# Where the stores wait: early stores on ScalarE's queue or held behind transposes, and a few softmax steps listed elsewhere

## The chip, the core and the metric

The kernel runs on one core of a Trainium2 chip. The metric is the device time of one execution in microseconds (us); the median of three runs of the kernel before is 420.4 us (419.74 to 420.79). The profile was taken on another execution of the same kernel, which took 418.92 us; its span from the first to the last instruction is 417.1 us, and all times inside the profile are counted from the start of that span.

The core has five engines with a queue of instructions each: TensorE (PE) multiplies matrices, VectorE (DVE) and ScalarE (ACT) do elementwise work, GpSimd (POOL) and SyncE (SP) here mainly start DMA transfers. A DMA can be started from the queues of SP, ACT or POOL.

## The reference, cut

```python
# 8 batches x 4160 positions x 192 channels (8 heads x 24 channels), kernel of 7 taps
w = exp(weight_gen - max(weight_gen, axis=-1))      # [B, S, 8, 7]
w = w / (sum(w, axis=-1) + 1e-09)
x_pad = concatenate([zeros(B, 6, D), x], axis=1)
x_unf = x_pad[:, idx, :].reshape(B, S, 7, 8, 24)    # position s sees s .. s + 6 of x_pad
out = einsum('bshk,bskhg->bshg', w, x_unf)          # a dynamic convolution
x = out.reshape(33280, 192)
g = maximum(x @ w1, x @ w2)                         # 192 -> 1024
result = g @ w_out                                  # 1024 -> 192, float32
```

The kernel writes maximum(h1, h2) as h1 + relu(h2 - h1): the hidden product is x @ (w2 - w1), then a relu, then its product with w_out, to which x @ (w1 @ w_out) is added.

## The kernel before: what the change touches

The 33,280 tokens are laid out as 128 partitions x 260 columns. The 260 columns form 17 *batches* b of 16 columns (the last has 4). DVE and the transposes work by *units* u: batches 0 and 1 have four units of 4 columns (u = 0 to 7), batches 2 to 15 two units of 8 columns (u = 8 to 35), batch 16 one unit of 4 (u = 36). The hidden products go by *tiles* t, one for each column (260), in *groups* g: pairs of tiles up to tile 15 (groups 0 to 7), then three tiles each (group 8 is tiles 16 to 18, group g is tiles 3g - 8 to 3g - 6). In each group two or four columns of the output are computed as well, some tiles behind.

For each batch the softmax is four steps on ACT and DVE, listed by hand at certain tiles: `exp_sum` (ACT), `red` (DVE), `ln` (ACT), `shift` (DVE), and `weights` (ACT), the final exp, once for each half-batch. Then DVE multiplies (`mul`) and adds (`adds`) to y. A DMA transposes y to yt, on SP's queue, and PE uses yt.

```python
    def exp_sum(b):                                              # ACT
        e_ts[b] = pe_.tile([P, BATCHES[b][1] * WGC], FP32, name="e_t", tag="e")
        nc.scalar.activation(out=e_ts[b], in_=wg_ts[b], func=AF.Exp)
    # ...
    def weights(b, o):                                           # ACT, line 158: en_t <- wg_t
        # ...
    def mul(b, o):                                               # DVE, line 173: m_t <- xb_t, en_t
        # ...
    def transpose(u):
        b, o, n = UNITS[u]
        yt = pyt.tile([P, 8 // 2 * 3 * P], BF16, name="yt", tag="yt")
        nc.sync.dma_start_transpose(                             # SP, line 207: yt <- y_t
            out=yt[:, 0:n // 2 * 3 * P].rearrange("p (b t) -> p b t", t=P),
            in_=y_ts[b][:, o * D:(o + n) * D],
        )
        yt_ts[u] = yt
        while held:
            held.pop(0)()

        nc.gpsimd.tensor_copy(out=gate, in_=yt[:, 0:1])          # POOL, line 215: waits for the landing
        c = b + 1 if o == 0 else b + 2
        if o == 8 and c < NB:
            load_x(c, 0, min(8, BATCHES[c][1]))
        if o == 0 and c < NB and BATCHES[c][1] > 8:
            load_x(c, 8, BATCHES[c][1] - 8)
        if o == 0 and b + 3 < NB:
            load_wg(b + 3, nc.gpsimd)
```

`transpose(u + 1)` is listed early in unit u, from unit 8 on (the first eight units are transposed by PE). The outputs are copied from PSUM by ACT and stored when a unit is complete:

```python
    def evac(p, n):
        # ... ACT, line 371: o_t <- op_ps, 24 columns of o_t are used in turn
        stores = []
        for q in range(p, p + n):
            u, i, _ = column(2 * q)
            if u < NU - 1 and i == UNITS[u][2] // 2 - 1:
                stores.append((nc.sync, place(q)[0] - i, [1, 2 * (i + 1) * D]))
            if u == NU - 1:
                stores.append((nc.sync, place(q)[0], [2 * D, 2], [1, D]))
        for eng, c, *ap in stores:
            def issue(eng=eng, c=c, ap=ap, o=o):
                eng.dma_start(                                   # line 383: out_dram <- o_t
                    # ...
                )
            if 8 <= u < NU - 3:
                held.append(issue)
            else:
                while held:
                    held.pop(0)()
                issue()
```

A group: PE does the hidden tiles but the last, then the first half of the outputs, then the last tile, then the second half. In a group with four output columns the listed steps (`beside`) come before the last relu and the eviction, in one with two after them:

```python
    def hidden(g, now=(), between=lambda: None, beside=lambda: None):
        t0, n = GROUPS[g]
        rd = room(g)
        for t in range(t0, t0 + n - 1):
            hid_tile(t)                                          # PE, line 275: hd <- yt, wd
        if now:
            out_room(now, "ab" if n == 1 and "ab" in ps else None)
            last = out_first(now)                                # PE, lines 327 and 315
        # ... relu of these tiles (ACT, line 285)
        hid_tile(t0 + n - 1)
        if len(now) > 2:
            beside()
        relu(rd, t0 + n - 1, 1)
        between()
        if now:
            out_second(now, go)                                  # PE, line 315
            evac(now[0] // 2, len(now) // 2)
        if len(now) <= 2:
            beside()
```

The tiles at which the softmax steps are listed, and the rule that puts off a long step in a group with four columns when the group before had a long one:

```python
    due = {}
    for c in range(3, NB):
        soon = c < 5
        parts_ = [(16 * (c - 2) + (8 if soon else 10), True, lambda c=c: weights(c, 0))]
        if 8 in dict(pieces(c)):
            parts_.append((16 * (c - 2) + (14 if soon else 15), True, lambda c=c: weights(c, 8)))
        if c > 3:
            ln_at = -2 if c == 4 else 0 if c < 8 else 2 if c < 11 else 4
            parts_.append((16 * (c - 2) + ln_at, False, lambda c=c: ln(c)))
            parts_.append((16 * (c - 3) + (4 if c == 4 else 7), True, lambda c=c: exp_sum(c)))
        for t, *step in parts_:
            due.setdefault(t, []).append(step)
    # ...
        two = len(OUTS[g]) <= 2
        put_off = [w for w in waiting if w[0] and not two and long_in_two[0]]
        now = [w for w in waiting if w not in put_off]
        waiting[:] = put_off
        for _, step in now:
            step()
        long_in_two[0] = two and any(long for long, _ in now)
```

Of the kernel before, what the change touches and what calls it, by code (L numbers as in the profile page):

```python
# [17 lines left out]
def _sub(base: bass.AP, off: int, dims):  # L18
    ap = [list(base.ap[0])] + [[int(s), int(c)] for s, c in dims]
    return dataclasses.replace(base, offset=base.offset + off, ap=ap)  # L20
# [3 lines left out]
def kernel(  # L24
# [9 lines left out]
    nc = tc.nc  # L34

    B, S, D = x.shape
# [13 lines left out]
    NB = len(BATCHES)  # L50


    def pieces(b):
        n = BATCHES[b][1]
        at, done = [], 0
        for w in (4, 4, 4, 4) if b < 2 else (8, 8) if n == 16 else (n,):
            at.append((done, w))
            done += w
        return at
# [65 lines left out]
    def exp_sum(b):  # L125
        e_ts[b] = pe_.tile([P, BATCHES[b][1] * WGC], FP32, name="e_t", tag="e")
        nc.scalar.activation(out=e_ts[b], in_=wg_ts[b], func=AF.Exp)  # L127
# [13 lines left out]
    def ln(b):  # L141
        nc.scalar.activation(out=s_ts[b], in_=s_ts[b], func=AF.Ln)  # L142
# [7 lines left out]
    def weights(b, o):  # L150

        w = dict(pieces(b))[o]
        if b not in en_ts:
            en_ts[b] = pen.tile([P, 16 * WGC * 2], BF16, name="en_t", tag="en")
        J = 2 if w == 4 and b < 2 else 1
        N = w * H // J
        for j in range(J):
            nc.scalar.activation(  # L158
                out=_sub(en_ts[b], (o * WGC + j * N * K) * 2, [[2 * N, K], [2, N], [1, 2]]),
                in_=_sub(wg_ts[b], (o * H + j * N) * K, [[1, K], [K, N], [0, 2]]), func=AF.Exp,  # L160
            )
# [90 lines left out]
    held = []  # L252
# [35 lines left out]
    def column(c):  # L288

        b = min(c // 16, NB - 1)  # L290
        for u, (ub, o, n) in enumerate(UNITS):
            if ub == b and o <= c - BATCHES[b][0] < o + n:
                k = c - BATCHES[b][0] - o
                return u, k // 2, k % 2

    def place(p):

        u, i, _ = column(2 * p)
        b, o, n = UNITS[u]
        return BATCHES[b][0] + o + i, n // 2  # L300
# [52 lines left out]
    def evac(p, n):  # L353

        tile_, at = op_at[p]
        o = o_t[0]
        if p == NT // 2 - 1:

            for j, copy, eng in ((0, nc.scalar.copy, nc.scalar), (1, nc.vector.tensor_copy, nc.sync)):
                c = place(p)[0] + 2 * j  # L360
                copy(out=o[:, c % 24 * D:(c % 24 + 1) * D], in_=tile_[:, at + j * 512:at + j * 512 + D])  # L361
                eng.dma_start(
                    out=bass.AP(tensor=out.tensor, offset=c * D, ap=[[CPP * D, P], [1, D]]),
                    in_=o[:, c % 24 * D:(c % 24 + 1) * D],
                )
            return
        runs = [[q for q in range(p, p + n) if column(2 * q)[0] == u]
                for u in range(column(2 * p)[0], column(2 * (p + n - 1))[0] + 1)]
        for qs in runs:
            c, h = place(qs[0])  # L370
            nc.scalar.copy(out=_sub(o, c % 24 * D, [[D, len(qs)], [h * D, 2], [1, D]]),  # L371
                           in_=_sub(tile_, at + (qs[0] - p) * D, [[D, len(qs)], [512, 2], [1, D]]))
        stores = []
        for q in range(p, p + n):
            u, i, _ = column(2 * q)
            if u < NU - 1 and i == UNITS[u][2] // 2 - 1:
                stores.append((nc.sync, place(q)[0] - i, [1, 2 * (i + 1) * D]))
            if u == NU - 1:
                stores.append((nc.sync, place(q)[0], [2 * D, 2], [1, D]))
        for eng, c, *ap in stores:  # L380

            def issue(eng=eng, c=c, ap=ap, o=o):
                eng.dma_start(
                    out=bass.AP(tensor=out.tensor, offset=c * D, ap=[[CPP * D, P], *ap]),
                    in_=_sub(o, c % 24 * D, ap),
                )

            if 8 <= u < NU - 3:
                held.append(issue)
            else:  # L390
                while held:
                    held.pop(0)()
                issue()

# [7 lines left out]
    OUTS, c = [[], [], []], 0  # L402
# [6 lines left out]
    NU = len(UNITS)  # L409
# [24 lines left out]
# [6 lines that stand above are left out]
            hid_tile(t)  # L440
        if now:
            out_room(now, "ab" if n == 1 and "ab" in ps else None)
            last = out_first(now)
        if len(now) > 2:
            relu(rd, t0, n - 1)
        else:
            for t in range(t0, t0 + n - 1):
                relu(rd, t, 1)
        if now:
            go = relay(last)  # L450
# [6 lines that stand above are left out]
            out_second(now, go)  # L457
# [4 lines that stand above are left out]
    def rest_of_results(c):  # L462

        parts = [p for p in (c[:4], c[4:-2], c[-2:]) if p]
        assert max(map(len, parts)) <= 4
        go = []
        for i, now in enumerate(parts):
            out_room(now, ("r", "ab", "c")[i])
            go.append(relay(out_first(now)))
            if i:  # L470
                out_second(parts[i - 1], go[i - 1])
                evac(parts[i - 1][0] // 2, len(parts[i - 1]) // 2)
        out_second(parts[-1], go[-1])
        evac(parts[-1][0] // 2, len(parts[-1]) // 2)
# [201 lines left out]

    due = {}
    for c in range(3, NB):
        soon = c < 5
        parts_ = [(16 * (c - 2) + (8 if soon else 10), True, lambda c=c: weights(c, 0))]  # L680
        if 8 in dict(pieces(c)):
            parts_.append((16 * (c - 2) + (14 if soon else 15), True, lambda c=c: weights(c, 8)))
        if c > 3:
            ln_at = -2 if c == 4 else 0 if c < 8 else 2 if c < 11 else 4
            parts_.append((16 * (c - 2) + ln_at, False, lambda c=c: ln(c)))
            parts_.append((16 * (c - 3) + (4 if c == 4 else 7), True, lambda c=c: exp_sum(c)))
        for t, *step in parts_:
            due.setdefault(t, []).append(step)
    waiting, long_in_two = [], [False]
# [87 lines left out]
```

The softmax here doesn't subtract the row's maximum and nothing guards it: scores larger than these inputs give would overflow.

## Time and profile before

| Engine | Busy us | Share of the span | Instructions |
|---|---|---|---|
| PE | 396.4 | 95% | 7369 |
| DVE | 377.2 | 90% | 218 |
| ACT | 359.2 | 86% | 424 |
| POOL | 84.2 | 20% | 102 |

| DMA issue | Queue | Count | KB each | Median us to landing |
|---|---|---|---|---|
| stores, 8 columns | SP | 28 | 768 | 4.9 |
| stores, 4 columns | SP | 8 | 384 | 2.6 |
| transposes yt <- y_t | SP | 29 | | 3.7 |

Busy time says how long an engine had an instruction under way; matmuls are pipelined, so a busy PE may still be waiting in part. The chain of waits in the profile puts 58% of the span on DVE and 24% on PE. In the profile, an engine's name with a q (SPq, ACTq) is its queue of DMA issues; a number in square brackets after an instruction is its engine's idle time before it, with what ended it. A line of the table of waits reads: who waited, for what, us in total, how often, the longest.

### The profile page before, as it was taken

The numbers are of one execution on the slowest core, as the hardware profiler recorded it, in microseconds if no ns is written. First come the engines' busy times: TensorE is split into PE (matmuls) and PEld (weight loads), VectorE is DVE, ScalarE is ACT, GpSimd is POOL, SyncE is SP. The second block draws the span as 40 slices with busy tenths as digits, with TensorE's granted clock in tenths as the row PEclk, the third lists the DMA queues.
The fourth block names the chain that finished last, engine by engine and source line by source line (L and its number), as shares of the span: only waits on it lengthen the run. The fifth ranks groups of instructions, "written<-read, shape, count | busy, mean of one in ns | idle before, by whom it ended". The sixth has DMA issues, their size and how long they took to land.

```text
span 417.1 us, 16029 instructions
## 1 busy us (share of the span) xinstructions
PE 396.4 (95%) x7369; PEld 320.9 (77%) x7369; DVE 377.2 (90%) x218; ACT 359.2 (86%) x424; POOL 84.2 (20%) x102
## 2 busy tenths in 40 slices
PE   7769899979999999999999999999999999989995
PEld 7668799767777778777787777777777777767795
DVE  5999999997989999999999999999999999999000
ACT  5888998969998999889898899998998989877871
POOL 1510101454113122220112222211221222210000
PEclk9999999999999999999999999999999999999999
DMA  8965425697663974766686587477639647544413
GB/s 249 258 166 160 108 78 79 152 191 195 158 143 73 269 181 77 238 178 123 115 240 168 123 220 174 103 204 206 140 92 256 164 64 235 151 87 116 172 55 137
DMA packets 60242, 65.68 MB, mean 157 GB/s; under 512 B 47601, under 2 KB 48497, under 8 KB 60176
## 3 DMA queue, kind: packets, MB, share of 16 engines
q1 hardware_dynamic: 51904, 40.47, 34.9%
q0 software_dynamic: 8128, 24.11, 27.9%
q8 instruction: 57, 0.93, 0.9%
q10 hardware_dynamic: 144, 0.10, 0.1%
q14 instruction: 9, 0.07, 0.1%
HBM read 35.96 MB, written 25.56 MB: 147 GB/s over the span
## 4 chain that ended last, share of the span: by engine, by line
DVE 58%; PE 24%; ACT 7%; issue 6%; DMA 4%; SPq 1%; DVEq 0%; ACTq 0%
DVE m_t L173 29%; DVE m_t L189 13%; PE op_ps L315 11%; PE hd L275 10%; DVE m_t L195 8%; ACT rd_t L285 3%; DVE sum_t L139 3%; DVE wg_t L147 2%; PE op_ps L327 2%; DVE y_t L198 2%; DMA yt<-y_t 2%; DMA ws1T<-in_moe_w_dram 2%; ACT en_t L158 1%; ACT yt L246 1%; ACT o_t L371 0%
## 5 line engine op out<-in xcount | busy, mean ns | idle before, releaser
L285 ACT ACTIVATE rd_t<-hd 128x1024 bf16<-128x1024 f32 (+1 forms) x206 | 234.7, 1188 | 29.8 <-PE hd L275 28.4
L315 PE MATMUL op_ps<-wo,rd_t 64*128 64x192 bf16 x4160 | 210.5, 243 | 0.1
L315 PEld LDWEIGHTS <-rd_t 64*128 64x128 bf16 x4160 | 180.4, 94 | 15.7 <-ACTq L348 0.3
L173 DVE TENSOR_TENSOR m_t<-xb_t,en_t 128x10752 bf16<-128x10752 bf16 (+1 forms) x37 | 187.5, 5069 | 4.0 <-ACT en_t L158 4.0
L275 PE MATMUL hd<-yt,wd 64*128 64x512 bf16 (+1 forms) x1584 | 187.5, 360 | 3.0 <-DMA yt<-y_t 2.2
L275 PEld LDWEIGHTS <-wd 64*128 64x128 bf16 x1776 | 94.2, 94 | 46.1 <-issue 5.9
L215 POOL CAST gate<-yt 128x1 f32<-128x1 bf16 x29 | 48.5, 1673 | 268.8 <-DMA yt<-y_t 268.8
L189 DVE TENSOR_TENSOR m_t<-m_t 128x4608 bf16<-128x4608 bf16 (+1 forms) x34 | 79.5, 2337 | 0.1
L371 ACT COPY o_t<-op_ps 128x384 f32<-128x384 f32 (+1 forms) x99 | 57.1, 590 | 12.8 <-PE op_ps L315 12.7
L327 PE MATMUL op_ps<-w,yt 64*128 64x192 bf16 x780 | 55.4, 243 | 5.2 <-ACT w L628 1.8
L327 PEld LDWEIGHTS <-yt 64*128 64x128 bf16 x780 | 38.3, 94 | 22.4 <-issue 7.2
L195 DVE TENSOR_TENSOR m_t<-m_t 128x3072 bf16<-128x3072 bf16 (+1 forms) x29 | 49.9, 1720 | 0.1
L158 ACT ACTIVATE en_t<-wg_t 128x896 bf16<-128x896 f32 (+2 forms) x45 | 34.9, 818 | 2.1 <-DVE wg_t L147 2.0
L198 DVE TENSOR_TENSOR y_t<-m_t 128x1536 bf16<-128x1536 bf16 (+1 forms) x29 | 27.2, 939 | 0.5
L361 DVE COPY o_t<-op_ps 128x192 f32<-128x192 f32 x1 | 0.4, 357 | 26.9 <-ACT o_t L361 26.9
L147 DVE TENSOR_TENSOR wg_t<-wg_t,sum_t 128x280 f32<-128x280 f32 (+4 forms) x45 | 21.9, 487 | 0.8 <-ACT sum_t L142 0.8
L115 POOL DMA_DIRECT2D xb_t<-in_x_dram x32 | 17.2, 538 | 23.5 <-DVE m_t L173 15.7
L139 DVE TENSOR_REDUCE sum_t<-e_t 128x64 f32<-128x448 f32 (+2 forms) x30 | 19.4, 648 | 2.4 <-ACT e_t L127 2.4
L127 ACT ACTIVATE e_t<-wg_t 128x896 f32<-128x896 f32 (+1 forms) x17 | 15.9, 936 | 2.3 <-DMA wg_t<-in_weight_gen_dram 2.3
L285 ACT ACTIVATE rd_t<-hdp 128x1024 bf16<-128x1024 f32 x16 | 15.9, 1026 | 1.2 <-PE hdp L275 1.0
L275 PE MATMUL hdp<-yt,wd 64*128 64x256 bf16 x192 | 13.1, 269 | 1.7 <-ACT yt L246 1.1
L590 PE MATMUL warm<-ident 128*128 128x128 bf16 x129 | 9.2, 243 | 3.0 <-DVE ident L529 3.0
(45 smaller groups left out, 79.7 us busy)
## 6 DMA issues: line engine op xcount, KB each, us to landing
out_dram<-o_t SPq DMA_DIRECT2D x28, 768.0 KB, 4.9
xb_t<-in_x_dram POOLq DMA_DIRECT2D x28, 384.0 KB, 5.0
wg_t<-in_weight_gen_dram POOLq DMA_DIRECT2D x14, 448.0 KB, 5.5
xb_t<-xb_t POOLq DMA_DIRECT2D x16, 288.0 KB, 5.6
out_dram<-o_t SPq DMA_DIRECT2D x8, 384.0 KB, 2.6
wg_t<-in_weight_gen_dram SPq DMA_DIRECT2D x2, 448.0 KB, 5.2
xs<-in_x_dram SPq DMA_DIRECT2D x2, 384.0 KB, 6.3
xb_t<-in_x_dram POOLq DMA_DIRECT2D x1, 768.0 KB, 6.8
```

What stands on the lines that cost most here:

```text
L139: nc.vector.reduce_sum(out=s_ts[b][:, hs], in_=_sub(e_ts[b], at, ap), axis=AX.X)
L158: nc.scalar.activation(out=_sub(en_ts[b], (o * WGC + j * N * K) * 2, [[2 * N, K], [2, N], [1, 2]]), in_=_sub(wg_ts[b], (o * H + j * N) * K ...
L173: nc.vector.tensor_tensor(out=m_out, in0=x_in, in1=_sub(en_ts[b], o * WGC * 2, [[2, K * n * H], [0, G // 2], [1, 2]]), op=ALU.mult,)
L189: nc.vector.tensor_tensor(out=taps(0, 1, 3), in0=taps(0, 1, 3), in1=taps(3, 1, 3), op=ALU.add)
L195: nc.vector.tensor_tensor(out=taps(0, 2, 2), in0=taps(0, 2, 2), in1=taps(1, 5, 2), op=ALU.add)
L198: nc.vector.tensor_tensor(out=_sub(y_ts[b], o * D, [[64, 2], [P, 3 * w // 2], [1, 64]]), in0=taps(0, 1, 1), in1=taps(2, 1, 1), op=ALU.add,)
L215: nc.gpsimd.tensor_copy(out=gate, in_=yt[:, 0:1])
L275: nc.tensor.matmul(hid_out(t, f, j), lhsT=wd[half(j), s * F + f * P:s * F + (f + 1) * P], rhs=_sub(yt_ts[u][half(j), :], (s + j) % 3 * P, ...
L285: nc.scalar.activation(out=rd[:, k * 1024:(k + n) * 1024], in_=hd[:, at:at + n * 1024], func=AF.Relu)
L315: return nc.tensor.matmul(op_out(c), lhsT=rd[half(r), k * 1024 + at:k * 1024 + at + P], rhs=wo[half(r), f * D:(f + 1) * D], start=False, s ...
L327: nc.tensor.matmul(op_out(c + j), lhsT=yt_ts[u][half(j), (3 * i + (s + j) % 3) * P:(3 * i + (s + j) % 3 + 1) * P], rhs=w10[half(j), s * D: ...
L371: nc.scalar.copy(out=_sub(o, c % 24 * D, [[D, len(qs)], [h * D, 2], [1, D]]), in_=_sub(tile_, at + (qs[0] - p) * D, [[D, len(qs)], [512, 2 ...
```

## The change

Three things are changed. The stores of units 0 to 3 (the first 16 columns) are issued from ACT's queue as soon as they are evicted. The stores of units 4 to 7, until now issued on SP's queue at once, are held and issued behind the next transpose, as those of the later units already were. And some softmax steps are listed at other tiles: those of batches 5 to 7 at earlier ones, the final exp of the last batch (16) five tiles later. The first two are to keep a store that waits for its eviction from standing ahead of a transpose in SP's queue; the third is to bring ACT's steps to where DVE needs them, and no sooner than DVE has prepared them.

```diff
@@ evac
             if u < NU - 1 and i == UNITS[u][2] // 2 - 1:
-                stores.append((nc.sync, place(q)[0] - i, [1, 2 * (i + 1) * D]))
+                stores.append((nc.scalar if u < 4 else nc.sync, place(q)[0] - i, [1, 2 * (i + 1) * D]))
@@ evac
-            if 8 <= u < NU - 3:
+            if 4 <= u < NU - 3:
                 held.append(issue)
             else:
-                while held:
+                while u > 3 and held:
                     held.pop(0)()
                 issue()
@@ due
     for c in range(3, NB):
-        soon = c < 5
-        parts_ = [(16 * (c - 2) + (8 if soon else 10), True, lambda c=c: weights(c, 0))]
+        soon = c < 8
+        parts_ = [(16 * (c - 2) + (8 if soon else 10 if c < NB - 1 else 15), True, lambda c=c: weights(c, 0))]
         if 8 in dict(pieces(c)):
             parts_.append((16 * (c - 2) + (14 if soon else 15), True, lambda c=c: weights(c, 8)))
         if c > 3:
             ln_at = -2 if c == 4 else 0 if c < 8 else 2 if c < 11 else 4
             parts_.append((16 * (c - 2) + ln_at, False, lambda c=c: ln(c)))
-            parts_.append((16 * (c - 3) + (4 if c == 4 else 7), True, lambda c=c: exp_sum(c)))
+            parts_.append((16 * (c - 3) + (4 if c < 8 else 7), True, lambda c=c: exp_sum(c)))
```

## The prediction

> **What bounds the kernel now.** I read the page's slices first. VectorE (DVE) is full until 386 us, TensorE (PE) nearly full from 50 us to the end, and ScalarE (ACT) at nine tenths.
>
> ```profile
> PE   7769899979999999999999999999999999989995
> PEld 7668799767777778777787777777777777767795
> DVE  5999999997989999999999999999999999999000
> ACT  5888998969998999889898899998998989877871
> ```
>
> A slice is 10.4 us. PE has one visible dent in the middle (the ninth digit, 83 to 94 us) and a small one near the end (the 36th); DVE has its dents in the tenth and twelfth slices, and then idles for the last 27 us while PE works on. The chain of waits goes along DVE from 122 to 368 us, so I first asked which of the two is really the bound, from their rates. In the timeline PE needs 0.65 us for the hidden matmuls of a tile and, for a pair of output columns, 0.25 + 0.66 + 0.66 us: 0.65 + 0.785 = 1.435 us per tile, 23.0 us per batch of 16. DVE needs 23.67 us (multiplications of one half-batch begin at 122.04 and, a batch later, at 145.71). DVE is slower per batch, but it has a lead: when PE begins tile 40 at 86.37 us, 220 tiles of hidden work and 228 columns of output are left, 220 x 0.65 + 228 x 0.785 = 322 us, and PE ends at 412.56, 326.2 us later. So only some 4 us of PE's last 326 us are not matmul work. PE is the bound, and what counts is each place where PE stood still. At the end DVE's lead is still about 3 us: y of the last full unit is written at 380.2, its transpose can have landed at about 384 (3.7 us is the median), and PE wants it at about 387.
>
> The table of waits names PE's stops and what DVE and ACT wait for:
>
> ```profile
> ACT en_t L158 <- DVE wg_t L147: 2.0, 1, 2.0
> PE hd L275 <- DMA yt<-y_t: 2.2, 1, 2.2
> DVE m_t L173 <- ACT en_t L158: 4.0, 3, 2.5
> PE op_ps L327 <- ACT o_t L371: 1.6, 3, 1.2
> ```
>
> The timelines of DVE, SyncE and PE around the first big stop (start, duration, engine, line):
>
> ```profile
> 58.18 0.95 DVE L198 TENSOR_TENSOR y_t<-m_t 128x1536 bf16<-128x1536 bf16 x1
> 65.81 1.97 SPq L207 DMA_TRANSPOSE yt<-y_t  x1
> 70.02 0.96 DVE L198 TENSOR_TENSOR y_t<-m_t 128x1536 bf16<-128x1536 bf16 x1
> 73.68 0.35 SPq L383 DMA_DIRECT2D out_dram<-o_t  x1
> 77.73 0.33 SPq L383 DMA_DIRECT2D out_dram<-o_t  x1
> 78.18 3.35 SPq L207 DMA_TRANSPOSE yt<-y_t  x1
> 86.37 1.47 PE L275 MATMUL hd<-yt,wd 64*128 64x512 bf16 x12 [2.16 <-DMA yt<-y_t]
> ```
>
> Unit 8's y is ready at 59.13, but its transpose is issued at 65.81: SyncE had been standing at unit 4's store, which waits for ACT's eviction. Unit 9's y is ready at 70.98; the stores of units 5 and 6 stand before its transpose, which goes out at 78.18, behind 768 KB of stores, and lands 8.06 us later. PE loses 2.16 us. The second loss:
>
> ```profile
> 368.34 0.62 ACT L158 ACTIVATE en_t<-wg_t 128x448 bf16<-128x448 f32 x1 [1.98 <-DVE wg_t L147]
> 370.66 0.42 PE L327 MATMUL op_ps<-w,yt 64*128 64x192 bf16 x6 [1.20 <-ACT o_t L371]
> ```
>
> The last batch's exp is listed on ACT before DVE's shift for it is done; ACT stands for 1.98 us, and PE behind it for 1.20 us.
>
> **What the Trainium skill says.** "DMA: Bandwidth & Descriptors", section on the anatomy of one DMA, says that a DMA's semaphore wait is served by the issuing sequencer before dispatch. The trace agrees: the transpose at 65.81 stood 6.7 us behind a store it has nothing to do with. The same page, "Issuing engines are not separate DMA queues", says that issuing from several engines saves only issue time, as all share the 16 DMA engines; so I expect no bandwidth from ACT's queue, only a free SyncE. The issue costs 0.34 us on SyncE and 0.37 us on ACT (the one at 412.94). "SBUF — State Buffer", "SBUF: two separate sides", says that GpSimd and a two-input DVE operation lock one another out. The trace agrees: the one-element gate copy that began at 71.68 ended at 76.69, the multiplication beside it at 76.65; the loads behind a transpose start only then. "Perfetto Trace Analysis", "Identifying the Most-Contended Engine", warns against matmul busy time; hence the sum from rates above.
>
> **The change part by part.**
> - Held stores, units 4 to 7. The order on SyncE becomes transpose 8, store 4, transpose 9, stores 5 and 6, transpose 10, store 7. Transpose 8 goes out at about 59.2, lands near 63.5 instead of about 71.6; transpose 9 at 71.0 instead of 78.18, landing near 75.5 instead of 86.23. PE would reach tile 40 at 86.37 - 2.16 = 84.2, so its 2.16 us wait is gone with 9 us to spare. The loads behind transpose 8 (x of batch 3, weights of batch 5) go out at about 65 instead of 76.6.
> - Stores of units 0 to 3 on ACT. They leave SyncE, but unit 3's would have been issued at about 60.4, so for transpose 8 this is worth about 1 us that nobody waits for. It adds 4 x 0.37 = 1.5 us to ACT. Those after the evictions at 52.58 and 59.95 fall in idle time of ACT (0.64 us there) or before a group with four columns, where PE has the longer work. Those at 36.8 and 44.9 lie where ACT is full and PE waits for it (0.77 us at 44.55, 0.89 at 49.20). Of these 0.74 us I count 0.4 on PE's path.
> - Softmax steps of batches 5 to 7. exp_sum(5) goes from group 15 to 14, so weights(4,0) is no longer put off and goes from group 17 to 16, a group of four columns; weights(5,0) goes from 23 to 21, exp_sum(6) from 21 to 20, exp_sum(7) from 26 to 25. DVE loses its waits of 2.54 us (at 97.18) and 1.10 us (at 122.04): 3.6 us. As PE is the bound, this is not gain in itself. On PE it takes away the stop of 0.35 us at 99.03 (0.46 by PE's cadence of that stretch) and the one at 126.61 (0.20; by cadence 0.33), both behind long steps on ACT: 0.8 us. It adds two others: a group of two columns gives PE 3 x 0.65 + 2 x 0.785 = 3.52 us and ACT three relus and an eviction, about 3.2 us, so one exp of 0.9 us more doesn't fit. exp_sum(5) now follows weights(3,8) in the next group, and weights(5,0) follows exp_sum(6): ACT's first three groups from 74.48 come to tile 40 at about 84.5 instead of 84.2 (-0.3), and the second pair costs about as much (-0.35).
> - weights(16,0) five tiles later, group 82 instead of 80: DVE's shift is then long done and the multiplication that needs it (380.13) still over 3 us away. PE gets 1.20 us.
>
> Sum: 2.16 - 0.3 + 0.8 - 0.35 + 1.20 - 0.4 = 3.1 us. 420.4 - 3.1 = 417.3 us, 0.7% less.
>
> **Rivals.**
> - DVE is the bound (the chain says so): then its 3.6 us count whole, and the two late microseconds of ACT don't; 416.8 us. Against it: PE has some 4 us of slack in 326, DVE waits for nothing at all from 123 to 386 and still leaves 27 us of PE work.
> - ACT takes over: its 1.5 us of issues and two long steps in neighbouring groups, with nothing hidden: the gain shrinks to about 1.5 us, 419 us. For it: ACT at nine tenths; PE's small waits before 100 us nearly all name ACT. Against: ACT's share there includes work that has slack in every four-column group.
> - A new wait on DVE: it comes 3.6 us earlier, PE and ACT only 3, so ln of batches 8 and 10 (done at 174.35 and 245.55 us, 0.7 and 0.5 us ahead of the shifts that need them) is met late. DVE then waits some tenths, with no effect on the end. If batch 4's weights come late because batch 5's wg is not there, ACT would stand: its load, by the step above, lands at about 71, and exp_sum(5) runs at about 81.
> - Transfers collide: transpose 9 now runs beside the loads behind transpose 8. Even at the 8.06 us seen before it lands at 79, 5 us early.
>
> **Range and chances.** Range 415.8 to 419.0: the lower end takes ACT's costs as hidden and the small slips (about 0.3 us, five times after 190 us) as gone in part; the upper is the second rival. 2% are 8.4 us, more than all of PE's stops after 50 us together; slower by that much would take a stall of a kind that I see no trace of. Faster 0.01, same 0.98, slower 0.01.
>
> **What would show it.** Transpose 8 issued right after 59.1 and 9 right after 71.0; no PE wait on yt; no DVE wait on en_t; PE at tile 40 at about 84.9 including the early 0.4; the DVE stream about 3 us earlier, PE's end at about 409.5; new PE waits on relu near 84 and 110 of a few tenths; no ACT wait on the last shift. It is wrong if PE ends earlier than its stops explain (DVE was the bound), if the stores on ACT cost more than 0.4 us each, or if PE's gain at tile 40 is lost again before the end.

## The result, and the profile after

The changed kernel takes 416.32 us (median of 6 runs, 415.67 to 417.38) beside 420.06 us of the kernel before (6 runs, 418.93 to 420.79): a ratio of 0.9914, with a 95% interval of 0.9892 to 0.9936. Taken again later (e9) it was 415.26 us beside 420.11 us, 0.9893 (0.9870 to 0.9917). Predicted were 417.3 us, within 415.8 to 419.0.

The page of the changed kernel, its slices and its chain of waits:

```profile
PE   7788899999999999999999999999999999999995
...
DVE  5999999999999999999999999999999999999000
ACT  5898989999988999889898899998999988988771
...
PE 81%; ACT 10%; issue 3%; DVE 2%; DMA 2%; SPq 1%; DVEq 0%; ACTq 0%
```

The dents of PE at 83 to 94 us and near 370 us are gone, and so are both dents of DVE. The chain, which gave DVE 58% before, now gives PE 81%: PE hardly ever lets go between 50 us and the end. The table of waits of the changed kernel (who waited, for what, us in total, times, longest):

```profile
DVE wg_t L147 <- ACT sum_t L142: 1.6, 3, 0.8
...
PE hd L275 <- ACT rd_t L285: 1.1, 4, 0.4
...
DVE m_t L173 <- ACT en_t L158: 0.3, 1, 0.3
```

PE no longer waits for yt (at one place with nothing to spare, see e6). DVE's 4.0 us of waits for en_t are 0.3 us; in their place it waits 0.8 us for ln of batch 8, the third rival of the prediction in its harmless form. The timelines of SyncE, PE and ACT at the places that the prediction named:

```profile
59.69 1.56 SPq L207 DMA_TRANSPOSE yt<-y_t  x1
65.85 0.36 SPq L383 DMA_DIRECT2D out_dram<-o_t  x1
71.46 1.42 SPq L207 DMA_TRANSPOSE yt<-y_t  x1
74.11 4.38 SPq L383 DMA_DIRECT2D out_dram<-o_t  x2
...
84.92 1.47 PE L275 MATMUL hd<-yt,wd 64*128 64x512 bf16 x12 [0.28 <-ACT rd_t L285]
...
373.09 0.62 ACT L158 ACTIVATE en_t<-wg_t 128x448 bf16<-128x448 f32 x1
```

Transposes 8 and 9 go out when their y is written, each with its stores behind it. PE starts tile 40 at 84.92 us with a wait of 0.28 us for a relu, and ACT's last exp has no bracket: nothing to wait for. PE's last matmuls end at about 409.4 us, against 412.6 before.

### The profile page after: what moved, and what is told of

It is laid out like the page before. It is cut to its first block, busy times and chain, and to the rows that moved or that the text cites. A ratio compares the mean times of both kernels' runs of the same rounds, so it can differ in the third digit from the quotient of the medians.

```text
span 413.9 us, 16025 instructions
## 1 busy us (share of the span) xinstructions
PE 397.5 (96%) x7369; PEld 322.9 (78%) x7369; DVE 377.3 (91%) x218; ACT 359.2 (87%) x424; POOL 73.5 (18%) x102
## 4 chain that ended last, share of the span: by engine, by line
PE 81%; ACT 10%; issue 3%; DVE 2%; DMA 2%; SPq 1%; DVEq 0%; ACTq 0%
PE op_ps L315 38%; PE hd L275 36%; PE op_ps L327 7%; ACT rd_t L285 6%; DMA ws1T<-in_moe_w_dram 2%; ACT en_t L158 1%; ACT yt L246 1%; DVE m_t L173 1%; ACT e_t L127 1%; ACT o_t L371 1%; PE hdp L275 0%; SPq L513 0%; ACT w1t L634 0%; DVE wd L549 0%; ACT w L628 0%
## 5 line engine op out<-in xcount | busy, mean ns | idle before, releaser
L275 PEld LDWEIGHTS <-wd 64*128 64x128 bf16 x1776 | 95.6, 94 | 42.9 <-issue 3.1
L215 POOL CAST gate<-yt 128x1 f32<-128x1 bf16 x29 | 38.0, 1312 | 277.4 <-DMA yt<-y_t 277.4
L275 PE MATMUL hdp<-yt,wd 64*128 64x256 bf16 x192 | 14.0, 284 | 1.2 <-ACT yt L246 1.1
```

The costliest lines, as they stand in the source:

```text
L275: nc.tensor.matmul(hid_out(t, f, j), lhsT=wd[half(j), s * F + f * P:s * F + (f + 1) * P], rhs=_sub(yt_ts[u][half(j), :], (s + j) % 3 * P, ...
```

## The experiments

Two theories were to be told apart. *PE's stops*: PE is the bound, and the time falls by what its stops at tile 40, near 370 us and behind long ACT steps were worth. *DVE's stream*: DVE is the bound, as the chain of before had it, and its 3.6 us of waits are the gain. A third question was what ACT's four issues cost.

| Run | Kernel | Median us (runs) | Ratio to before, 95% interval | PE at tile 40, us | Last PE result taken by ACT, us |
|---|---|---|---|---|---|
| | before (first profile) | 420.06 (6) | | 86.37 | 412.59 |
| e9 | changed | 415.26 (6) | 0.9893 (0.9870 to 0.9917) | 84.42 | 408.92 |
| e1 | before + both store parts | 416.70 (6) | 0.9912 (0.9882 to 0.9941) | 83.79 | 410.06 |
| e12 | before + stores of units 5, 6 held | 416.62 (6) | 0.9929 (0.9905 to 0.9953) | 83.92 | 410.20 |
| e2 | before + softmax steps 5 to 7 | 419.66 (22) | 0.9967 (0.9948 to 0.9985) | 87.33 | 412.86 |
| e3 | before + last exp later | 418.78 (12) | 0.9949 (0.9925 to 0.9974) | 87.46 | 412.17 |
| e4 | changed, units 0 to 3 on SP | 415.15 (5) | 0.9862 (0.9835 to 0.9889) | 84.44 | 408.76 |
| e10 | the same again | 415.86 (6) | 0.9898 (0.9876 to 0.9919) | 86.16 | 410.44 |
| e5 | changed, last exp back | 416.83 (6) | 0.9912 (0.9878 to 0.9945) | 84.45 | 409.82 |
| e6 | changed + 1.6 us on DVE | 417.66 (14) | 0.9940 (0.9916 to 0.9964) | 85.72 | 414.05 |
| e7 | changed + 1.95 us on PE | 417.92 (17) | 0.9944 (0.9925 to 0.9963) | 86.07 | 412.33 |
| e8 | changed, steps spread | 414.39 (5) | 0.9869 (0.9829 to 0.9909) | 84.04 | 407.90 |
| e11 | spread, units 0 to 3 on SP | 414.19 (5) | 0.9864 (0.9841 to 0.9887) | 85.52 | 409.30 |

The kernel before, run beside each set, took 420.70 us (33 runs, beside e1 to e4), 420.50 us (30, e5 to e8) and 420.11 us (11, e9 to e12); the ratios are to these. The medians of one kernel scatter by about 1 us from one set of runs to another, so where less is at stake I go by the places in the traces, that is by the last two columns and their difference. (Tile 40 at 85.5 to 86.2 in e6, e7, e10 and e11 comes from a slow stretch of PE's clock before 46 us, told in the last section.)

**e1: the store part alone.**

```diff
# the kernel before, plus
+                stores.append((nc.scalar if u < 4 else nc.sync, place(q)[0] - i, ...))
+            if 4 <= u < NU - 3:
+                while u > 3 and held:
```

> The kernel before with the store part alone (units 0 to 3 on ACT's queue, units 4 to 7 held). Theory (PE's own stops set the time): the 2.16 us wait for yt at tile 40 goes, nothing else; exp_sum(5) stays in group 15, so no new stop there. PE starts tile 40 about 2.1 us earlier, the stops at the next long steps (0.35 us then, 0.2 us near 124) and the late one of 1.2 us stay: about 2.1 us less than before, 418.0. DVE's wait for en_t of 2.54 us shrinks to about 0.5 us, because ACT comes earlier, without any step being moved. Rival (ACT takes over, its four issues count whole): 1.5 us of the gain are lost, 419.4.

PE starts tile 40 at 83.79 us without a wait, 2.6 us earlier than in the profile of before (0.26 us of it from a start that was earlier already at 32 us). From there to the end it takes 326.3 us, and 326.2 before: the store part shortens nothing but the way to tile 40. The DVE timeline shows what comes free with it, and the PE timeline what stays:

```profile
94.62 5.76 DVE L173 TENSOR_TENSOR m_t<-xb_t,en_t 128x10752 bf16<-128x10752 bf16 x1 [0.24 <-ACT en_t L158]
119.48 5.76 DVE L173 TENSOR_TENSOR m_t<-xb_t,en_t 128x10752 bf16<-128x10752 bf16 x1 [1.10 <-ACT en_t L158]
...
368.14 0.42 PE L327 MATMUL op_ps<-w,yt 64*128 64x192 bf16 x6 [1.06 <-ACT o_t L371]
```

DVE's wait of 2.54 us falls to 0.24 us although no softmax step was moved: it was a follow-up of PE's stop, which had held up ACT. DVE thereby writes y of its last full unit at 377.7 us instead of 380.2, so this run alone doesn't tell the two theories apart. The median fell by 4.0 us, more than the trace accounts for; see the last section.

**e12: only the two stores ahead of transpose 9 held.**

```diff
# the kernel before, with
-            if 8 <= u < NU - 3:
+            if 8 <= u < NU - 3 or u in (5, 6):
```

> The kernel before with only the stores of units 5 and 6 held (they stood ahead of transpose 9); unit 4's still stands ahead of transpose 8, unit 7's ahead of transpose 10. Theory (the one wait for transpose 9 is the whole worth of the store part): transpose 8 goes out at 65.8 as before, transpose 9 at 71.0, PE's wait at tile 40 is gone, and the time is that of the store part alone, 416.7 to 418. Rival (transpose 8 and the loads behind it matter too): between that and the kernel before.

SyncE's timeline:

```profile
65.20 0.33 SPq L383 DMA_DIRECT2D out_dram<-o_t  x1
65.64 1.87 SPq L207 DMA_TRANSPOSE yt<-y_t  x1
70.89 1.50 SPq L207 DMA_TRANSPOSE yt<-y_t  x1
73.51 0.34 SPq L383 DMA_DIRECT2D out_dram<-o_t  x1
```

Transpose 8 is as late as ever, behind unit 4's store, but transpose 9 goes out right after its y, written at 70.81 us. Tile 40 starts at 83.92, and the median is that of e1. Holding two stores gives the whole worth of the store part; transpose 8's six microseconds were on nobody's path here. PE waits once more, 0.47 us at 291.54 us for the transpose of unit 27, a wait that the kernel before doesn't have.

**e2: the softmax steps of batches 5 to 7 alone.**

```diff
# the kernel before, with
-        soon = c < 5
+        soon = c < 8
-            parts_.append((16 * (c - 3) + (4 if c == 4 else 7), True, lambda c=c: exp_sum(c)))
+            parts_.append((16 * (c - 3) + (4 if c < 8 else 7), True, lambda c=c: exp_sum(c)))
```

> The kernel before with the softmax steps of batches 5 to 7 at the new tiles, and nothing else. Theory (PE): the wait for yt of 2.16 us at tile 40 stays; the stops near 99 and 126 us go (0.8 us), one near 110 comes (0.35); DVE's two waits for en_t go, but DVE then meets ln of batches 8 and 10, which hang on PE and ACT, and keeps only about 1 us of its 3.6; the late stop falls from 1.2 to about 0.75 us: 0.9 us less in all, 419.2. Rival (DVE is the bound and its waits for en_t count): 3.6 us less, 416.5.

The median, 419.66 us, is where PE's stops put it and 3 us from the other number; with its ratio of 0.9967 (0.9948 to 0.9985) it is a small gain. The timelines of ACT, PE and DVE show that these steps don't stand alone:

```profile
83.82 0.95 ACT L127 ACTIVATE e_t<-wg_t 128x896 f32<-128x896 f32 x1 [1.96 <-DMA wg_t<-in_weight_gen_dram]
...
87.33 1.47 PE L275 MATMUL hd<-yt,wd 64*128 64x512 bf16 x12 [2.48 <-DMA yt<-y_t]
...
98.61 5.76 DVE L173 TENSOR_TENSOR m_t<-xb_t,en_t 128x10752 bf16<-128x10752 bf16 x1 [3.85 <-DMA xb_t<-xb_t]
```

exp_sum(5), listed earlier, stands 1.96 us for weights that are loaded only behind the late transpose 8, and DVE's wait for en_t has become one for x, loaded behind the late transpose 9. I had expected DVE's waits to vanish here; they were replaced, and y of the last full unit comes at 380.5 us (380.2 before). So DVE won nothing in this run, and it doesn't test DVE's theory. From tile 40 to the end PE takes 325.5 us, 0.7 less than before, and the late stop is still 1.08 us.

**e3 and e5: the last exp, alone and taken back.**

```diff
# e3: the kernel before, with (e5: the changed kernel, the other way round)
-        parts_ = [(16 * (c - 2) + (8 if soon else 10), True, lambda c=c: weights(c, 0))]
+        parts_ = [(16 * (c - 2) + (8 if soon else 10 if c < NB - 1 else 15), True, lambda c=c: weights(c, 0))]
```

> The kernel before with the exp of the last batch five tiles later, and nothing else. Theory (PE): the 1.20 us stop near 370 us goes: 418.9. Rival (DVE): DVE's stream is the same, no gain: 420.1.

> The changed kernel with the exp of the last batch back at its old tile. Theory (PE): ACT comes to it at about 364.5 us and the last shift ends at 366.0; ACT stands for about 1.6 us and PE behind it for about 0.8: 0.8 us slower than the changed kernel, 417.1. Rival (DVE): the same as the changed kernel, 416.3.

e3's median is 418.78 us, where PE's stop puts it; but the kernel before took 420.70 us beside it, so the gain is 1.9 us and not 1.2. In its trace, tile 40 was later than in the profile of before (a wait for yt of 3.39 us), and from there PE takes 412.17 - 87.46 = 324.7 us instead of 326.2: 1.5 us, of which the stop was 1.20. In e5 the wait returns, shorter, because DVE has gained on ACT; its ACT and PE timelines:

```profile
365.57 0.62 ACT L158 ACTIVATE en_t<-wg_t 128x448 bf16<-128x448 f32 x1 [1.56 <-DVE wg_t L147]
...
367.90 0.42 PE L327 MATMUL op_ps<-w,yt 64*128 64x192 bf16 x6 [0.78 <-ACT o_t L371]
```

1.56 us for ACT and 0.78 us for PE, with 1.6 and 0.8 expected. The end comes at 409.82 against 408.92 in e9: 0.9 us. DVE writes y of its last full unit at 377.5 us in e5 as in e9, so DVE's theory has no room for this 0.9.

**e4 and e10: ACT's issues taken back.**

```diff
# the changed kernel, with
-                stores.append((nc.scalar if u < 4 else nc.sync, place(q)[0] - i, ...))
+                stores.append((nc.sync, place(q)[0] - i, ...))
```

> The changed kernel with the stores of units 0 to 3 back on SP's queue, at once, as before. The prediction counted 0.4 us for the issues on ACT: then this one is 0.4 us faster than the changed kernel (415.9). The trace of the changed kernel says that PE was late by 0.45 us before the first of these stores and by 0.48 us behind the second, so that they cost next to nothing: then the same as the changed kernel, 416.3, with transpose 8 about 1.2 us later (behind unit 3's store at about 61) and nobody waiting for it. Rival (ACT takes over): 1.5 us faster, 414.8.

> The changed kernel with the stores of units 0 to 3 back on SP's queue, again, beside the changed kernel. If ACT's issues cost PE nothing, as the traces say: the same within 0.3 us. If they cost what the prediction counted: 0.4 us less. If the 1.2 us between the two medians so far is real: 1.2 us less.

e4 came out 1.2 us below the first set of runs of the changed kernel, which looked like a cost of ACT's issues. Its trace said otherwise (408.76 us at the end, 408.92 in e9), and side by side on one chip, e9 and e10, the order turned round: 415.26 with, 415.86 without, intervals overlapping. The four issues are there in the ACT timeline of e9:

```profile
36.77 0.37 ACTq L383 DMA_DIRECT2D out_dram<-o_t  x1
44.90 0.34 ACTq L383 DMA_DIRECT2D out_dram<-o_t  x1
53.09 0.34 ACTq L383 DMA_DIRECT2D out_dram<-o_t  x1
60.42 0.34 ACTq L383 DMA_DIRECT2D out_dram<-o_t  x1
```

In the same trace PE's stops at 44.54 and 49.19 us are 0.78 and 0.90 us, and 0.77 and 0.89 us in the kernel before, at 44.55 and 49.20: the issues at 36.77 and 44.90 lengthened neither. This part of the change is worth nothing and costs nothing that can be measured.

**e7 and e6: more work on PE, more work on DVE.**

```diff
# e7: the changed kernel, with; the tiles' results are written twice
         for t in range(t0, t0 + n - 1):
-            hid_tile(t)
+            for _ in range(2 if t in (160, 166, 172) else 1):
+                hid_tile(t)
# e6: the changed kernel, with; the same sums are taken four times
-            beside=lambda i, of: red(b + 3, i, 2) ...
+            beside=lambda i, of: [red(b + 3, i, 2) for _ in range(4 if b + 3 == 13 and i == 0 else 1)] ...
```

> The changed kernel with the hidden matmuls of tiles 160, 166 and 172 done twice (the second time overwrites the first): 3 x 0.65 = 1.95 us more on PE. Theory (PE is the bound): 1.95 us more, 418.3. Rival (DVE is the bound): the same as the changed kernel, 416.3.

> The changed kernel with the first half of the sums of batch 13 done four times instead of once on DVE (the same result each time): 3 x 0.53 = 1.6 us more on DVE, in the middle of the stretch in which DVE never idles. Theory (PE is the bound, DVE has some 2 to 3 us of lead at the end): the same as the changed kernel, 416.3. Rival (DVE is the bound): 1.6 us more, 417.9.

e7 bears the theory out: the median is 417.92 us, and in the trace PE is 1.16 us behind the first profile of the changed kernel at 195.34 us (against 194.18) and 2.95 us behind at 294.76 (against 291.81): 1.8 us of the added 1.95, and all of it is still there at the end (412.33 against 409.39). (This execution was late by the 1.16 us before the first doubled tile.)

e6 does not: 417.66 us, when nothing should have happened. The reason is not that DVE is the bound all along. The PE timeline of e6 and its windows at that place (length, busy time of PE, PEld, DVE, ACT and POOL, granted clock of PE, DMA share, GB/s):

```profile
349.68 0.83 PE L275 MATMUL hd<-yt,wd 64*128 64x512 bf16 x6
352.55 1.46 PE L275 MATMUL hd<-yt,wd 64*128 64x512 bf16 x6 [2.04 <-DMA yt<-y_t]
```

```profile
348.00:350.00 2.00, 2.00 (x42) 1.69 (x40) 2.00 (x1) 1.67 (x3) 0.00 (x0) 1.00 0.90 169
350.00:352.00 2.00, 0.50 (x6) 0.10 (x2) 2.00 (x1) 0.69 (x1) 0.00 (x0) 1.00 1.12 407
352.00:354.00 2.00, 1.45 (x10) 0.70 (x11) 2.00 (x3) 0.00 (x0) 0.72 (x2) 0.64 0.96 396
354.00:356.00 2.00, 2.00 (x27) 1.75 (x24) 2.00 (x3) 1.89 (x2) 0.00 (x0) 0.51 0.88 135
```

Tile 224, the first of unit 32, had to wait for its transpose; it was the only wait of PE for yt. How much earlier than needed a transpose lands, its lead, is read from two places: the gate copy on POOL, which starts at the landing, and PE's pair of tiles whose second is the first of the unit, 0.65 us into the pair. At unit 32, in the changed kernel (e9):

```profile
348.11 1.75 POOL L215 CAST gate<-yt 128x1 f32<-128x1 bf16 x1 [9.06 <-DMA yt<-y_t]
...
348.37 1.48 PE L275 MATMUL hd<-yt,wd 64*128 64x512 bf16 x12
```

The lead is 348.37 + 0.65 - 348.11 = 0.9 us; in the kernel before it was 350.72 + 0.65 - 350.84 = 0.5 us. It is thinnest at unit 29 (tiles 199 and 200), whose transpose lands 5.3 us after its y in the kernel before and 5.7 us after it in e9. The kernel before:

```profile
316.76 0.38 POOL L215 CAST gate<-yt 128x1 f32<-128x1 bf16 x1 [10.46 <-DMA yt<-y_t]
...
315.73 1.78 PE L275 MATMUL hd<-yt,wd 64*128 64x512 bf16 x12
```

And e9:

```profile
314.34 0.40 POOL L215 CAST gate<-yt 128x1 f32<-128x1 bf16 x1 [10.81 <-DMA yt<-y_t]
...
313.67 1.48 PE L275 MATMUL hd<-yt,wd 64*128 64x512 bf16 x12
```

In e9 the lead is 313.67 + 0.65 - 314.34 = 0.0 us. In the kernel before it is 315.73 + 0.65 - 316.76 = -0.4 us: PE waited, and the pair takes 1.78 us instead of 1.47, a stop of 0.3 us that the table of waits doesn't list.

e6 used up the lead with 1.6 us on DVE and, at unit 32, a transpose that took 5.5 us to land (y written at 347.0, wait over at 352.55) instead of 3.9 (344.2 to 348.1). PE stood 2.04 us and then lost 1.6 us more because it ran at about half its clock for some 4 us. This traced execution is the slowest of the 14 (420.34 us), so most of the others lost less. The kernel is bound by PE, but the transposes come just in time, so that e6's 1.6 us on DVE show in the median as e7's 1.95 us on PE do.

**e8 and e11: the long steps spread.**

```diff
# the changed kernel, with (e11: and units 0 to 3 on SP)
-        parts_ = [(... (8 if soon else 10 if c < NB - 1 else 15), True, lambda c=c: weights(c, 0))]
+        parts_ = [(... (8 if c < 5 else 10 if c < NB - 1 else 15), 2 if c in (4, 8, 11, 14) else 1, lambda c=c: weights(c, 0))]
-                          (4 if c < 8 else 7), True, lambda c=c: exp_sum(c)
+                          (4 if c in (4, 6, 7) else 7), True, lambda c=c: exp_sum(c)
-        put_off = [w for w in waiting if w[0] and not two and long_in_two[0]]
+        put_off = [w for w in waiting if w[0] == 1 and not two and long_in_two[0]]
```

> The changed kernel with no two long softmax steps in one group or in neighbouring groups: exp_sum(5) back in group 15 with weights(4,0) still in group 16; weights(5,0) in group 22; weights of batches 8, 11 and 14 in groups 38, 54 and 70 (of four columns), not beside those of the second half. Theory (PE's small stops behind ACT): the stops of 0.28 us near 85 and 110 us go, and three slips of about 0.3 us: up to 1.5 us less than the changed kernel, 414.8 to 415.5. Rival (these slips come from elsewhere): the same, 416.3.

> The spread softmax steps with the stores of units 0 to 3 on SP's queue: no two long steps in one group or neighbouring groups, and nothing on ACT's queue before the end. If ACT's issues cost nothing: as the spread kernel, 414.4. If they cost 0.4 to 1.2 us: 413.2 to 414.0.

414.39 and 414.19 us, the lowest medians of the study. In the trace e8 ends 1.0 us before e9. The ACT timelines show one of the places: in e9 both halves of batch 8's weights stand in one group, in e8 one of them.

```profile
188.03 1.99 ACT L158 ACTIVATE en_t<-wg_t 128x896 bf16<-128x896 f32 x2
```

```profile
187.65 1.06 ACT L158 ACTIVATE en_t<-wg_t 128x896 bf16<-128x896 f32 x1
```

Behind the first, PE stood 0.21 us at 193.70; behind the second it doesn't stand. The stop near 85 us is gone too, but that of 0.27 us near 109 stays: with weights(5,0) moved away it can't have been the pair. It comes with exp_sum(6) alone in group 20, a group of two columns with another one behind it. The gain over the changed kernel is 1 us by the traces; the intervals of the ratios overlap, so by the medians alone it is likely, not certain. (e11 and e10, both with units 0 to 3 on SP and run on one chip, differ by 1.7 us in their medians and by 0.5 us in their traces from tile 40 on.)

## Why the prediction was right

**The bound.** Right in kind: the stop at tile 40 (e12), the stop near 370 us (e3 and e5) and 1.95 us of added work (e7) each move the end by about their length. e1 and e2 alone don't decide against DVE: in e1 it won as much as PE (2.5 us), in e2 nothing. The step that failed is "at the end DVE's lead is still about 3 us": it was read at unit 35 (387.2 - 384.5 = 2.7 us), but at unit 32 the lead is 0.5 us in the kernel before and 0.9 us in the changed one, and at unit 29 there is none, -0.4 and 0.0 us. The last batch has 4 columns, so DVE's sums and shifts for it are short (0.26 and 0.21 us instead of 0.61 and 0.44), and the lead opens again before unit 35. It follows that "this is not gain in itself" was too strong for DVE: with the transposes at their old times, PE could not have begun tile 200 before 316.7 us, whatever it had gained until then (2.1 us in e9). The prediction got the sum right because transpose 29 landed earlier as well, by 2.4 us in e9. It did expect DVE to be about 3 us earlier, but did not see that its sum needed it; to that extent the right sum was luck.

**Held stores.** Right: transpose 8 at 59.69 and 9 at 71.46 were predicted for 59.2 and 71.0 (the run was 0.4 us late before), and the 2.16 us are gone. e12 narrows it: two stores do it.

**Stores on ACT.** "I count 0.4 on PE's path" is wrong; counted from the start at 32 us, PE is 0.1 us later near 44.5 us with these issues than without (12.59 us in e9, 12.51 in e4), and at tile 40 nothing is left of it (84.42 and 84.44 us). That tile 40 began at 84.92, as predicted, was chance in this term: that execution was 0.45 us late at 32 us, before the first of these stores. In e9 it begins at 84.42.

**Softmax steps 5 to 7.** The stop at 99 us went and one of 0.28 us came at tile 40 (predicted 0.3) and one of 0.28 us near 110 (predicted 0.35). The place was right, the reason of the last was not: not the pair with weights(5,0), but exp_sum(6) alone (e8). That DVE's wait at 97 us was removed by moving steps is also not shown: the stores alone left 0.24 us of it (e1), and the steps alone replaced it by a wait for x (e2). What these steps are worth beside the store parts follows from e5, which is e1 with them added: from PE's start at 32 us to the end e1 takes 378.3 us and e5 377.9, so 0.4 us by one trace each, where the terms of the prediction make 0.15 (0.8 - 0.3 - 0.35). The medians, 416.70 and 416.83 us, don't show it.

**The last exp.** Counted at 1.20 us, it is worth 1.5 in e3 and 0.9 in e5, since the rest of the change shortens the wait.

**The sum.** Without the 0.4 us for ACT the prediction's terms make 3.5 us; between the first profile of before and e9 the end moved by 3.7 us, and by 3.6 us net of the start. The medians say 3.7 and 4.9 us.

## What to carry to other kernels

In a queue that serves transfers on the critical path and transfers that nobody waits for, a store that is issued "at once" holds up everything listed behind it until its own data are there (transpose 8 stood 6.7 us behind one here); list it behind the transfer that matters, and look for the two or three places where it counts. Read the engine that bounds from rates and stops over the whole stretch, not from the chain alone, and read the lead of the engine behind it at every hand-over: its smallest value, not the last, says how much of the next gain will come through. A wait that ends on another engine may be only the echo of a stop elsewhere, so remove the stop first and look again before moving steps.

## What the runs showed of the hardware that I had not expected

A stop of PE can cost more than its length. After the 2.04 us in e6 the granted clock was 0.64 and 0.51 in the next two windows of 2 us, and 1.6 us more were lost. The same happens early: PE stands 1.83 us before 32 us in nearly every run; in the trace of e10 the clock was then 0.59 and 0.56 for 4 us and all behind it came 1.4 us later (46.23 instead of 44.54 us, 0.27 of these 1.7 us there before), in e9 it was 1.00. All seven slow stretches before the end of PE's work in the fourteen traces (two in e6, one each in e7, e10, e11, e12 and the first profile of the changed kernel) come right behind a stop of 1.8 to 2.3 us. But most such stops, and the one of 3.39 us in e3, were followed by a clock of 1.00, so it isn't the length alone; what decides was not tested.

The medians fall by more than the traces when PE's stop at tile 40 goes (4.0 us in e1, with 2.3 in its trace). A slow clock behind that stop would fit, but none was traced. Two other reasons are as good: the stop is not the same each time (2.16, 2.48 and 3.39 us in before, e2 and e3, the three traces that have it), and the profiled execution of before, 418.92 us, lies 1.1 to 1.8 us below its medians. Which of them it is stays open.
